# Backward decode attention: dV outer products and the next step's sums interleaved on TensorE, V products made a half quarter ahead

## The chip, the cores and the metric

The kernel runs on one core of a Trainium2 chip. Its time is the device time of one launch in microseconds; lower is better. Five engines work side by side, each taking its own instructions in order: TensorE (PE in the profile, PEld its weight loads), VectorE (DVE), ScalarE (ACT), GpSimd (POOL, used here to issue stores and one kind of load) and SyncE (SP, which issues loads). 16 DMA engines move the data between main memory (HBM) and the on-chip memory (SBUF). TensorE writes into PSUM, from where VectorE and ScalarE read.

## What is computed

One decoding step of a conditioned transformer block, with its gradients. The reference, cut to what matters (all data in bfloat16):

```python
# D = 640, 32 heads, 8192 keys, head size 192
def A_ref(x, k, v, wq, wo):                       # attention, one query row per head
    q = (x @ wq).reshape(B, Sq, 32, 192).transpose(0, 2, 1, 3)
    p = softmax(einsum('bhqd,bhkd->bhqk', q, k) * 192 ** -0.5)
    o = einsum('bhqk,bhkd->bhqd', p, v)
    return o.transpose(0, 2, 1, 3).reshape(B, Sq, 6144) @ wo
mod = (silu(c) @ w_mod).reshape(1, 6, 1, 640)     # sa, ca, ga, sb, cb, gb
x = x + ga * A_ref(layernorm(x) * (1 + ca) + sa, k_cache, v_cache, wq, wo)
x = x + gb * B_ref(layernorm(x) * (1 + cb) + sb)  # a small MLP block
out, vjp = jax.vjp(f, x, k_cache, v_cache, wq, wo, w3, w4, c, w_mod)
return out, *vjp(grad_out)
```

For one head with softmax weights p, output gradient do and query q, the backward pass needs, for every key j: dP_j = V_j . do (a dot product over 192 elements), dS_j = p_j (dP_j - const), dK_j = dS_j q and dV_j = p_j do. The gradients of the caches are as large as the caches: 32 heads x 8192 keys x 192, 100 MB each. V is read a second time for dP; K isn't, since the forward pass keeps what dQ needs.

## The kernel before, in words

The forward part runs over the heads and takes the first 550 us or so. A short chain of small operations follows (the MLP block and its gradients). Then comes the loop to which the change belongs.

**The backward loop.** It has 64 steps (`NS = 2 * HQ`), one for half of the keys of one head, 4096 keys laid out as 128 partitions x 32 keys (`JH`), in two quarters of 16 keys (`JQ`). What a step s does:

- `dot_sum(ps, dP)` (L314, DVE): adds up the last 16 partial sums per key that lie in PSUM: dP of this step. Then dS in one operation (L1156), each value four times.
- `mul_q(s + 1, q)` (L855, DVE): V times do for quarter q of the *next* step, into half q of the buffer `pq`. `tree_q(ps, q)` (L864, PE): 12 matmuls with the identity as weights, which add the 192 products of a key down to 16 in PSUM. One buffer `dot_ps` holds both quarters.
- `dv_groups` (L875, PE): dV. Eight groups a step; each is four matmuls with one row of p as the weights (outer products with do), into one of two PSUM buffers `dv_ps`, and one eviction by ScalarE (L876, 128x768) into a bfloat16 buffer.
- `dk_part` (L880, DVE): dK, in two halves.
- `dv_store` (L1126) and the dK store (L1197) are issued by POOL, as is `load_er` (L704), which fetches the rows of p for step s + 2 into one of two buffers `er_b`. It has to wait until PE is done with the groups of step s. V for step s + 4 is loaded by SP (L295) into one of three buffers, as soon as its last reader, the products of step s + 1, is done.
- dV and dK go into five buffers (named `KB` in the profile, `OB` in the code) that are used in turn.

**Side jobs.** A step has four calls of `slot()`. Each runs a share of a list of small pieces of work: the transposes and products for dWq, dW_mod and dWo, and `g_do`, which makes do of later heads from rows of wo. How many pieces are due by which slot is fixed by a formula; there is no planner. A chunk of dWq or dW_mod goes through `g_chunk` in five pieces: a cast (L943), transposes of a weight chunk (L746, evicted by ACT at L747) together with the transpose of three small rows (L948) and their copy `vrow` (L950), more transposes with a broadcast (L955, evicted at L957), matmuls (L962) with three row products (L964), and an addition (L966) with the last two row products (L968). The loads of weight chunks go through SP (L904, L214), their stores through POOL (L972, L999).

**What sets the order.** The order of the instructions on PE, DVE, ACT and SP is that of the program text (`manual_schedule`); the framework adds the waits that the data need. POOL issues its transfers in the order of the text too. An engine whose next instruction has to wait holds up everything behind it.

The step in the old order: dot_sum, dS, slot, groups 0 to 3, product 0 and its tree, slot, first half of dK, groups 4 and 5, slot, groups 6 and 7, load of er_b, store of dV, product 1 and its tree, V load, second half of dK, store of dK, slot.

Of the kernel before, what the change touches and what calls it, by code (L numbers as in the profile page):

```python
# [10 lines left out]
ALU = mybir.AluOpType  # L11
# [9 lines left out]
def kernel(  # L21
# [26 lines left out]
    nc = tc.nc  # L48
    P = 128
    D = A_x.shape[-1]  # L50
    _, HQ, S, DH = A_k_cache.shape
# [4 lines left out]
    JH = J // 2  # L56
    JQ = J // 4
    TS = 16
    TF = 8
    HW = DH // 2  # L60
    ND = D // P
# [232 lines left out]
    def load_v(h, t, v):  # L294
        nc.sync.dma_start(out=v, in_=V_hd[h][:, t * JH : (t + 1) * JH, :])  # L295
        return v
# [410 lines left out]
    def ht(s):  # L707

        return H1 - s // 2, (1 - s % 2 if s < 2 else s % 2)
# [29 lines left out]
    def transposed(x0, cols, outer, wT):  # L739

        n = min(8, 15 - x0)
        tp = psT.tile([P, 1024], BF16, name="wT_ps", tag="t")
        for x in range(x0, x0 + n):
            b, a = divmod(x, outer)
            for lo, hi, src in cols(a, b):
                T_.transpose(out=tp[lo:hi, (x - x0) * P : (x - x0 + 1) * P], in_=src, identity=ident_bf)  # L746
        A_.copy(out=wT[:, x0 * P : (x0 + n) * P], in_=tp[:, 0 : n * P])  # L747
# [7 lines left out]
    def do_mm(t, b=None):  # L755
        wT = woT[t]
        ps = psB.tile([P, 512], FP32, name="do_ps", tag="b")
        bs = (0, 1) if b is None else (b,)
        w = DH * len(bs)
        for i in range(ND):  # L760
            rhs = wT[:, i * PW : (i + 1) * PW].rearrange("p (c a) -> p c a", c=3)[:, :, 64 * bs[0] : 64 * bs[-1] + 64]
            T_.matmul(ps[:, 0:w], lhsT=dao_bf[:, i : i + 1].to_broadcast([P, P]), rhs=rhs, start=(i == 0), stop=(i == ND - 1))  # L762
        for k, b in enumerate(bs):
            h = 2 * t + b
            A_.activation(
                out=do_of(h).rearrange("p (a c) -> p a c", c=3),
                in_=ps[:, 0:w].rearrange("p (c a) -> p a c", c=3)[:, 64 * k : 64 * k + 64, :],
                func=ACT.Copy,
                scale=rinv[:, h : h + 1],
            )  # L770
# [83 lines left out]
    def mul_q(s, q):  # L854
        V_.tensor_tensor(  # L855
            out=pq[:, q],
            in0=v_l[s][:, q * JQ : (q + 1) * JQ, :],
            in1=do_of(ht(s)[0])[:, None, :].to_broadcast([P, JQ, DH]),
            op=ALU.mult,
        )  # L860

    def tree_q(ps, q):
        for k in range(0, DH, TS):
            T_.matmul(ps[:, q * JQ : (q + 1) * JQ, :], lhsT=ident_bf, rhs=pq[:, q, :, k : k + TS], start=(k == 0), stop=(k == DH - TS), skip_group_check=True)  # L864

    def dv_groups(dV, er, doh, gs):

        dV4 = dV.rearrange("p (r k) d -> p r (k d)", r=4)
        for g in gs:
            m, q = divmod(g, 2)  # L870
            ps = psV.tile([P, 2, 512], FP32, name="dv_ps", tag="v")
            for k in range(2):
                for b in range(2):
                    p0 = 32 * (2 * q + b)
                    T_.matmul(ps[:, b, k * DH : (k + 1) * DH], lhsT=er[p0 : p0 + 1, 2 * m + k, :], rhs=doh[p0 : p0 + 1, :], start=True, stop=True)  # L875
            A_.copy(out=dV4[:, 2 * q : 2 * q + 2, m * PW : (m + 1) * PW], in_=ps[:, :, 0:PW])  # L876

    def dk_part(dK, qh, dS4, lo, hi):
        n = hi - lo
        V_.tensor_tensor(  # L880
            out=dK[:, lo:hi, :].rearrange("p j (a b) -> p j a b", b=4),
            in0=qh.rearrange("p (a b) -> p a b", b=4)[:, None, :, :].to_broadcast([P, n, DH // 4, 4]),
            in1=dS4[:, lo:hi, None, :].to_broadcast([P, n, DH // 4, 4]),
            op=ALU.mult,
        )
# [49 lines left out]
    def g_chunk(b, first, v3, rows, dst, n, acc, lay):  # L935

        lo = n * CW
        if first:
            cur["w"] = cur.pop("next")
        w = stg = cur["w"][:, :, b * PW : (b + 1) * PW]  # L940
        cols = lambda a, b_: [(l, r, w[:, a, c0 : c0 + r - l]) for bb, l, r, c0 in lay if bb == b_]
        v_bf = tcol(3, "v_bf", BF16)
        V_.tensor_copy(out=v_bf, in_=v3)  # L943
        yield
        wT = bst.tile([P, 15 * P], BF16, name="wT", tag="wT")
        transposed(0, cols, ND, wT)
        tp = psS.tile([NF, P], FP32, name="bc_t", tag="s")
        T_.transpose(out=tp[0:3, :], in_=v3, identity=ident_f)  # L948
        vrow = tmp.tile([3, P], BF16, name="vrow")
        V_.tensor_copy(out=vrow, in_=tp[0:3, :])  # L950
        yield
        transposed(8, cols, ND, wT)
        bp = psB.tile([P, 512], FP32, name="bc_ps", tag="b")
        for bb, l, r, c0 in lay:
            T_.matmul(bp[:, c0 : c0 + r - l], lhsT=pick(3, bb), rhs=vrow[:, l:r], start=True, stop=True)  # L955
        v_bc = bst.tile([P, PW], BF16, name="v_bc")
        A_.copy(out=v_bc, in_=bp[:, 0:PW])  # L957
        yield
        ps = psS.tile([P, ND], FP32, name="acc_ps", tag="s")
        for i in range(ND):  # L960
            for bb in range(3):
                T_.matmul(ps[:, i : i + 1], lhsT=wT[:, (bb * ND + i) * P : (bb * ND + i + 1) * P], rhs=v_bf[:, bb : bb + 1], start=(bb == 0), stop=(bb == 2))  # L962
        for i in range(3):
            V_.tensor_scalar(out=stg[:, i, :], in0=v_bc, scalar1=rows[:, i : i + 1], scalar2=None, op0=ALU.mult)  # L964
        yield
        V_.tensor_tensor(out=acc, in0=ps, in1=acc, op=ALU.add)  # L966
        for i in range(3, ND):
            V_.tensor_scalar(out=stg[:, i, :], in0=v_bc, scalar1=rows[:, i : i + 1], scalar2=None, op0=ALU.mult)  # L968
        if first:
            next_w()  # L970
        else:
            nc.gpsimd.dma_start(out=dst[:, :, lo : lo + CW], in_=cur["w"])  # L972
        yield
# [118 lines left out]
    def slot():  # L1092
        prog[0] += 1
        k = prog[0] - 1
        due = sum(n for i, n in RAMP.items() if i <= k) if k < R0 else NR + -(-(NP - NR) * (k - R0 + 1) // (SLOTS - R0))
        while prog[1] < min(due, NP):
            next(side)
            prog[1] += 1

    def v_buf(s):  # L1100
        return KY if s == 0 else VB[(s + 1) % NVB]
# [39 lines left out]
    dw4_store(stg0[:, 2 * D :], 9, 3)  # L1141
    V_.tensor_tensor(out=cpr, in0=c_ps, in1=rinv, op=ALU.mult)
    tree_q(ps, 1)
    V_.memset(dha, 0.0)
    V_.memset(dsc, 0.0)
    row = None
    for s in range(NS):
        h, t = ht(s)
        nxt = s + 1 < NS
        doh = do_of(h)  # L1150
        qh = qs_bc[:, h * DH : (h + 1) * DH]
        assert not nxt or (s + 1) // 4 in done
        dP = tcol(JH, "dP")
        dot_sum(ps, dP)
        dS4 = bst.tile([P, JH, 4], BF16, name="dS4", bufs=2)
        V_.scalar_tensor_tensor(  # L1156
            out=dS4,
            in0=dP[:, :, None].to_broadcast([P, JH, 4]),
            scalar=cpr[:, h : h + 1],
            in1=E_all[:, h, t * JH : (t + 1) * JH, None].to_broadcast([P, JH, 4]),  # L1160
            op0=ALU.subtract,
            op1=ALU.mult,
        )
        slot()
        dV, dK = OB[(2 * s) % len(OB)], OB[(2 * s + 1) % len(OB)]
        if s == 0:
            dv_groups(dV, er, doh, (1, 3))
            do_mm(TL, 0)
        else:
            er = er_l.pop(s)  # L1170
            dv_groups(dV, er, doh, (0, 1, 2, 3))
        if nxt:
            ps = psR.tile([P, JH, TS], FP32, name="dot_ps")
            mul_q(s + 1, 0)
            tree_q(ps, 0)
        if row is not None:
            dq_cols(row)
            row = None
        slot()
        dk_part(dK, qh, dS4, 0, JQ)  # L1180
        if s > 0:
            dv_groups(dV, er, doh, (4, 5))
        slot()
        dv_groups(dV, er, doh, (5, 7) if s == 0 else (6, 7))
        if s + 2 < NS:
            er_l[s + 2] = load_er(s + 2)
        dv_store(s, dV, JQ if s == 0 else 0, JH)
        if nxt:
            mul_q(s + 1, 1)
            tree_q(ps, 1)  # L1190
            v_l.pop(s, None)
        if h == H1:
            row = dq_rows(t, (KD, KE)[t], dS4)
        if s + 4 < NS:
            v_l[s + 4] = load_v(*ht(s + 4), v_buf(s + 4))
        dk_part(dK, qh, dS4, JQ, JH)
        nc.gpsimd.dma_start(out=dK_hd[h][:, t * JH : (t + 1) * JH, :], in_=dK)  # L1197
        done_s[0] = s + 1
        slot()
    while prog[1] < NP:  # L1200
# [32 lines left out]
```

## Time and profile before

| what | value |
|---|---|
| time, median of 3 runs | 1435.73 us (1430.34 to 1438.45) |
| the profiled execution's own time | 1433.26 us |
| its span, first to last instruction | 1431.5 us |
| PE busy | 1105.0 us (77%) |
| DVE busy | 1104.2 us (77%) |
| ACT busy | 871.5 us (61%) |
| bytes moved by DMA | 569.38 MB, mean 398 GB/s |
| mean granted TensorE clock | 0.768 |

How to read it: the page gives, for each engine, the time in which it was busy, and for the span in 40 slices the busy share of each engine in tenths, the TensorE clock that was granted, and what the DMA engines moved. The other views answer for a stretch of the span: busy time and transfer rate by stretch, groups of instructions by line with the idle time ahead of them and what ended it, waits by pair of waiter and awaited, and the instructions in order of time. The first step of the backward loop starts near 593 us, the last one ends near 1420 us.

### The profile page before, as it was taken

To read this page: it belongs to the slowest core of one execution; us is meant where nothing else is said; L and a number is where in the kernel's file an instruction comes from. 1 tells how busy PE (TensorE), PEld (TensorE's weight loads), DVE (VectorE), ACT (ScalarE), POOL (GpSimd) and SP (SyncE) were. 2 spreads that over 40 slices of the span, in tenths; PEclk is the share of its full clock that TensorE was granted. 3 is DMA by queue.
4 is the path that set the end of the run, shared out by engine and by line. 5 is a ranking of instruction groups with operands and counts; after the bars stand their busy time and mean duration, and the time that the engine had idled before them with its cause. 6 is when DMAs were issued, how large, how long until landed. Compare 5 with 4: busy or idle time off the path is not lost.

```text
span 1431.5 us, 30396 instructions
## 1 busy us (share of the span) xinstructions
PE 1105.0 (77%) x12744; PEld 790.1 (55%) x12744; DVE 1104.2 (77%) x1410; ACT 871.5 (61%) x1953; POOL 145.6 (10%) x254
## 2 busy tenths in 40 slices
PE   3988889999999998767757677677777777666864
PEld 2777777777777777634334344444444444344532
DVE  4989999999999996676757677676676676667674
ACT  0767777777777775455646466555565556455554
POOL 0000000000000000111211111111111111111111
PEclk9999999999999998766667575666655555556565
DMA  9999999999999995499999999999999999999998
GB/s 374 391 397 418 415 417 417 412 422 411 420 408 413 418 415 211 164 385 428 422 399 425 427 408 421 416 425 403 425 418 425 402 422 414 358 385 382 422 404 372
DMA packets 77417, 569.38 MB, mean 398 GB/s; under 512 B 8766, under 2 KB 26510, under 8 KB 36958
## 3 DMA queue, kind: packets, MB, share of 16 engines
q1 hardware_dynamic: 50842, 340.44, 59.2%
q0 software_dynamic: 26416, 226.97, 38.0%
q8 instruction: 100, 1.64, 0.5%
q14 instruction: 39, 0.32, 0.1%
q10 hardware_dynamic: 20, 0.00, 0.0%
HBM read 340.95 MB, written 226.43 MB: 396 GB/s over the span
## 4 chain that ended last, share of the span: by engine, by line
PE 26%; DVE 12%; DMA 8%; ACT 8%; issue 4%; POOL 1%; ACTq 0%; POOLq 0%; DVEq 0%; SPq 0%
PE dot_ps L864 17%; DVE pq L855 6%; ACT KB L876 6%; DMA wo_st<-in_A_wo_dram 4%; PE wT_ps L746 3%; PE dv_ps L875 3%; DMA stg<-in_A_wq_dram 2%; ACT wT L747 2%; DMA out_dram<-wo_st 2%; DVE dP L314 2%; DVE KB L880 1%; DMA out_dram<-stg 1%; PE do_ps L762 1%; DVE dq_junk L984 1%; DVE dS L1156 0%
## 5 line engine op out<-in xcount | busy, mean ns | idle before, releaser
L876 ACT CAST KB<-dv_ps 128x768 bf16<-128x768 f32 x512 | 376.3, 815 | 146.9 <-PE dv_ps L875 146.5
L864 PE MATMUL dot_ps<-pq,ident_bf 128*128 128x256 bf16 x1536 | 317.2, 388 | 50.2 <-DVE pq L855 50.1
L357 ACT ACTIVATE vs<-VB,Ef 128x192 bf16<-128x192 bf16 x872 | 314.9, 447 | 0.0
L864 PEld LDWEIGHTS <-ident_bf 128*128 128x128 bf16 x1536 | 198.5, 133 | 146.2 <-issue 77.4
L875 PE MATMUL dv_ps<-do_r,er_b 1*128 1x192 bf16 x2048 | 173.5, 309 | 131.1 <-ACT KB L876 129.9
L300 DVE TENSOR_TENSOR prod<-KB,qs_bc 128x6144 bf16<-128x6144 bf16 x62 | 207.9, 3353 | 30.0 <-DMA KB<-in_A_k_cache_dram 23.0
L880 DVE TENSOR_TENSOR KB<-qs_bc,dS 128x3072 bf16<-128x3072 bf16 x128 | 223.8, 1749 | 4.5 <-DMA out_dram<-KB 4.2
L855 DVE TENSOR_TENSOR pq<-VB,do_r 128x3072 bf16<-128x3072 bf16 x126 | 220.3, 1749 | 0.0
L372 PE MATMUL mp<-vs,KB 128*128 128x193 bf16 x1984 | 191.3, 249 | 4.3 <-ACT vs L357 2.8
L747 ACT COPY wT<-wT_ps 128x1024 bf16<-128x1024 bf16 x84 | 81.0, 964 | 185.4 <-PE wT_ps L746 185.4
L875 PEld LDWEIGHTS <-er_b 1*128 1x128 bf16 x2048 | 65.7, 102 | 223.2 <-issue 220.4
L372 PEld LDWEIGHTS <-KB 128*128 128x128 bf16 x1984 | 171.2, 98 | 13.6 <-DMA KB<-in_A_k_cache_dram 4.7
L310 PE MATMUL half_ps<-prod,ident_bf 128*128 128x256 bf16 x744 | 95.1, 279 | 45.8 <-DVE prod L304 45.4
L314 DVE TENSOR_REDUCE dP<-dot_ps 128x32 f32<-128x512 f32 x64 | 44.0, 688 | 109.8 <-PE dot_ps L864 109.8
L350 DVE TENSOR_TENSOR vs<-VB,E 128x1728 bf16<-128x1728 bf16 (+1 forms) x122 | 127.1, 1062 | 0.3 <-ACT vs L357 0.3
L304 DVE TENSOR_TENSOR prod<-prod 128x3072 bf16<-128x3072 bf16 x62 | 108.7, 1753 | 1.0
L310 PEld LDWEIGHTS <-ident_bf 128*128 128x128 bf16 x744 | 72.8, 99 | 64.1 <-issue 55.0
L377 PE MATMUL mp<-vs,KB 128*64 128x193 bf16 x1984 | 108.0, 252 | 0.0
L377 PEld LDWEIGHTS <-KB 128*64 128x64 bf16 x1984 | 80.8, 111 | 19.8 <-issue 19.7
L337 ACT ACTIVATE E<-S_h,negm 128x256 bf16<-128x256 f32 x31 | 15.8, 508 | 116.0 <-DVE negm L498 113.7
L704 POOL DMA_DIRECT2D er_b<-eT_d x64 | 37.3, 583 | 476.1 <-PE dv_ps L875 474.3
L432 POOL DMA_DIRECT2D eT_d<-er x16 | 8.8, 548 | 560.1 <-ACT vs L348 519.7
(270 smaller groups left out, 1008.5 us busy)
## 6 DMA issues: line engine op xcount, KB each, us to landing
out_dram<-KB POOLq DMA_DIRECT2D x127, 1536.0 KB, 15.6
VB<-in_A_v_cache_dram SPq DMA_DIRECT2D x123, 1536.0 KB, 11.6
KB<-in_A_k_cache_dram SPq DMA_DIRECT2D x64, 1536.0 KB, 11.6
wo_st<-in_A_wo_dram SPq DMA_DIRECT2D x31, 480.0 KB, 12.1
w_st<-in_A_wq_dram SPq DMA_DIRECT2D x12, 960.0 KB, 13.5
out_dram<-wo_st POOLq DMA_DIRECT2D x16, 480.0 KB, 18.8
out_dram<-w_st POOLq DMA_DIRECT2D x7, 960.0 KB, 16.4
w_st<-in_w_mod_dram SPq DMA_DIRECT2D x6, 960.0 KB, 18.2
```

Of the source, the lines that this page charges most:

```text
L300: V_.tensor_tensor(out=prod, in0=src, in1=vec[:, None, :].to_broadcast([P, JH, DH]), op=ALU.mult)
L310: T_.matmul(ps, lhsT=ident_bf, rhs=prod[:, :, k : k + TF], start=(k == 0), stop=(k == w - TF))
L350: V_.tensor_tensor(out=vs[:, 0:n, 0:DH].rearrange("p j (a b) -> p j a b", b=4), in0=v[:, v0 : v0 + n, :].rearrange("p j (a b) -> p j a b", ...
L357: A_.activation(out=vs[:, k, 0:DH], in_=v[:, v0 + k, :], func=ACT.Copy, scale=Ef[:, j0 + k : j0 + k + 1])
L372: T_.matmul(mp[:, 0:MW], lhsT=kb[:, j0 + k, 0:P], rhs=vs[:, k, 0:MW], start=(q == 0 and k == 0), stop=(z and k == JQ - 1), skip_group_chec ...
L377: T_.matmul(mp[p0 : p0 + 64, MO : MO + MW], lhsT=kb[:, j0 + k, P:DH], rhs=vs[:, k, 0:MW], start=False, stop=(z and k >= JQ - 2), skip_grou ...
L747: A_.copy(out=wT[:, x0 * P : (x0 + n) * P], in_=tp[:, 0 : n * P])
L855: V_.tensor_tensor(out=pq[:, q], in0=v_l[s][:, q * JQ : (q + 1) * JQ, :], in1=do_of(ht(s)[0])[:, None, :].to_broadcast([P, JQ, DH]), op=AL ...
L864: T_.matmul(ps[:, q * JQ : (q + 1) * JQ, :], lhsT=ident_bf, rhs=pq[:, q, :, k : k + TS], start=(k == 0), stop=(k == DH - TS), skip_group_c ...
L875: T_.matmul(ps[:, b, k * DH : (k + 1) * DH], lhsT=er[p0 : p0 + 1, 2 * m + k, :], rhs=doh[p0 : p0 + 1, :], start=True, stop=True)
L876: A_.copy(out=dV4[:, 2 * q : 2 * q + 2, m * PW : (m + 1) * PW], in_=ps[:, :, 0:PW])
L880: V_.tensor_tensor(out=dK[:, lo:hi, :].rearrange("p j (a b) -> p j a b", b=4), in0=qh.rearrange("p (a b) -> p a b", b=4)[:, None, :, :].to ...
```

## The change

Within a step, the order of the work on the engines changes; no operation is added or taken away.

- Each dV group on PE is followed by some of the sums of the next step: four matmuls each after groups 1, 2 and 3 (quarter 0), three each after groups 4 to 7 (quarter 1). `tree_q` takes the range as arguments.
- Product 0 is made two steps ahead, at the end of the step (`mul_q(s + 2, 0)`, and `mul_q(1, 0)` ahead of the loop); product 1 of the next step is made after the first slot.
- The load of V for step s + 4 follows product 1, ahead of groups 2 to 7.
- Both halves of dK come in the middle of the step, and its store is issued there, ahead of the er_b load and the store of dV.
- The first step, of which four groups were made ahead of the loop, has its other four at places 0, 1, 4 and 6.
- In `g_chunk` the three small rows are transposed ahead of the wide transposes, their copy `vrow` moves to the next piece, and all five row products stand in the last piece.

```diff
@@ -859,8 +859,8 @@
             op=ALU.mult,
         )
 
-    def tree_q(ps, q):
-        for k in range(0, DH, TS):
+    def tree_q(ps, q, lo=0, hi=DH // TS):
+        for k in range(lo * TS, hi * TS, TS):
             T_.matmul(ps[:, q * JQ : (q + 1) * JQ, :], lhsT=ident_bf, rhs=pq[:, q, :, k : k + TS], start=(k == 0), stop=(k == DH - TS), skip_group_check=True)
 
     def dv_groups(dV, er, doh, gs):
@@ -943,12 +943,12 @@
         V_.tensor_copy(out=v_bf, in_=v3)
         yield
         wT = bst.tile([P, 15 * P], BF16, name="wT", tag="wT")
-        transposed(0, cols, ND, wT)
         tp = psS.tile([NF, P], FP32, name="bc_t", tag="s")
         T_.transpose(out=tp[0:3, :], in_=v3, identity=ident_f)
+        transposed(0, cols, ND, wT)
+        yield
         vrow = tmp.tile([3, P], BF16, name="vrow")
         V_.tensor_copy(out=vrow, in_=tp[0:3, :])
-        yield
         transposed(8, cols, ND, wT)
         bp = psB.tile([P, 512], FP32, name="bc_ps", tag="b")
         for bb, l, r, c0 in lay:
@@ -960,11 +960,9 @@
         for i in range(ND):
             for bb in range(3):
                 T_.matmul(ps[:, i : i + 1], lhsT=wT[:, (bb * ND + i) * P : (bb * ND + i + 1) * P], rhs=v_bf[:, bb : bb + 1], start=(bb == 0), stop=(bb == 2))
-        for i in range(3):
-            V_.tensor_scalar(out=stg[:, i, :], in0=v_bc, scalar1=rows[:, i : i + 1], scalar2=None, op0=ALU.mult)
         yield
         V_.tensor_tensor(out=acc, in0=ps, in1=acc, op=ALU.add)
-        for i in range(3, ND):
+        for i in range(ND):
             V_.tensor_scalar(out=stg[:, i, :], in0=v_bc, scalar1=rows[:, i : i + 1], scalar2=None, op0=ALU.mult)
         if first:
             next_w()
@@ -1141,6 +1139,7 @@
     dw4_store(stg0[:, 2 * D :], 9, 3)
     V_.tensor_tensor(out=cpr, in0=c_ps, in1=rinv, op=ALU.mult)
     tree_q(ps, 1)
+    mul_q(1, 0)
     V_.memset(dha, 0.0)
     V_.memset(dsc, 0.0)
     row = None
@@ -1149,7 +1148,6 @@
         nxt = s + 1 < NS
         doh = do_of(h)
         qh = qs_bc[:, h * DH : (h + 1) * DH]
-        assert not nxt or (s + 1) // 4 in done
         dP = tcol(JH, "dP")
         dot_sum(ps, dP)
         dS4 = bst.tile([P, JH, 4], BF16, name="dS4", bufs=2)
@@ -1161,40 +1159,62 @@
             op0=ALU.subtract,
             op1=ALU.mult,
         )
-        slot()
         dV, dK = OB[(2 * s) % len(OB)], OB[(2 * s + 1) % len(OB)]
+        gs = [0, 1, 2, 3, 4, 5, 6, 7]
         if s == 0:
-            dv_groups(dV, er, doh, (1, 3))
-            do_mm(TL, 0)
+            gs = [1, 3, None, None, 5, None, 7, None]
         else:
             er = er_l.pop(s)
-            dv_groups(dV, er, doh, (0, 1, 2, 3))
         if nxt:
             ps = psR.tile([P, JH, TS], FP32, name="dot_ps")
-            mul_q(s + 1, 0)
-            tree_q(ps, 0)
+
+        def dv(k):
+            if gs[k] is not None:
+                dv_groups(dV, er, doh, (gs[k],))
+
+        def tree(q, lo, hi):
+            if nxt:
+                tree_q(ps, q, lo, hi)
+
+        dv(0)
+        dv(1)
+        slot()
+        if s == 0:
+            do_mm(TL, 0)
+        tree(0, 0, 4)
+        if nxt:
+            mul_q(s + 1, 1)
+            v_l.pop(s + 1, None)
+        if s + 4 < NS:
+            v_l[s + 4] = load_v(*ht(s + 4), v_buf(s + 4))
+        dv(2)
+        tree(0, 4, 8)
+        dv(3)
+        tree(0, 8, 12)
         if row is not None:
             dq_cols(row)
             row = None
+        dk_part(dK, qh, dS4, 0, JQ)
         slot()
-        dk_part(dK, qh, dS4, 0, JQ)
-        if s > 0:
-            dv_groups(dV, er, doh, (4, 5))
+        dv(4)
+        tree(1, 0, 3)
+        dk_part(dK, qh, dS4, JQ, JH)
+        nc.gpsimd.dma_start(out=dK_hd[h][:, t * JH : (t + 1) * JH, :], in_=dK)
+        dv(5)
+        tree(1, 3, 6)
         slot()
-        dv_groups(dV, er, doh, (5, 7) if s == 0 else (6, 7))
+        dv(6)
+        tree(1, 6, 9)
+        dv(7)
         if s + 2 < NS:
             er_l[s + 2] = load_er(s + 2)
         dv_store(s, dV, JQ if s == 0 else 0, JH)
-        if nxt:
-            mul_q(s + 1, 1)
-            tree_q(ps, 1)
-            v_l.pop(s, None)
+        tree(1, 9, 12)
         if h == H1:
             row = dq_rows(t, (KD, KE)[t], dS4)
-        if s + 4 < NS:
-            v_l[s + 4] = load_v(*ht(s + 4), v_buf(s + 4))
-        dk_part(dK, qh, dS4, JQ, JH)
-        nc.gpsimd.dma_start(out=dK_hd[h][:, t * JH : (t + 1) * JH, :], in_=dK)
+        if s + 2 < NS:
+            assert (s + 2) // 4 in done
+            mul_q(s + 2, 0)
         done_s[0] = s + 1
         slot()
     while prog[1] < NP:
```

## The prediction

> **What bounds the kernel now.** The page first: its span and, of the 40 slices, the share of time for which the 16 DMA engines were busy (tenths) and what they moved.
>
> ```profile
> span 1431.5 us, 30396 instructions
> DMA  9999999999999995499999999999999999999998
> GB/s 374 391 397 418 415 417 417 412 422 411 420 408 413 418 415 211 164 385 428 422 399 425 427 408 421 416 425 403 425 418 425 402 422 414 358 385 382 422 404 372
> ```
>
> The change lies in the backward loop, slices 17 to 40. DMA is busy in all of them, but the rate wanders between 358 and 428 GB/s. So the second view is busy time by stretches: the start of the loop, its body, a stretch at the best rate, a long stretch, a stall, a late stretch and the tail.
>
> ```profile
> 592.00:640.00 48.00, 32.02 (x346) 20.62 (x345) 36.34 (x36) 28.76 (x43) 7.74 (x14) 0.82 0.87 328
> 640.00:1420.00 780.00, 555.55 (x4595) 335.77 (x4593) 543.81 (x782) 437.81 (x614) 124.28 (x211) 0.62 1.00 411
> 660.00:680.00 20.00, 15.08 (x113) 8.83 (x113) 13.22 (x13) 11.31 (x18) 2.19 (x4) 0.59 1.01 427
> 964.00:1200.00 236.00, 175.73 (x1455) 107.68 (x1454) 164.85 (x248) 136.44 (x193) 36.28 (x61) 0.61 1.01 416
> 1217.50:1237.60 20.10, 9.62 (x84) 5.45 (x83) 10.22 (x20) 6.82 (x9) 2.79 (x5) 0.50 0.86 344
> 1240.00:1380.00 140.00, 101.73 (x860) 62.46 (x858) 101.76 (x168) 76.75 (x106) 22.12 (x36) 0.59 1.00 394
> 1420.00:1431.50 11.50, 0.00 (x0) 0.00 (x0) 0.00 (x0) 0.00 (x0) 0.70 (x2) 0.50 0.68 284
> ```
>
> Columns after the length: busy PE, PEld, DVE, ACT, POOL, then granted clock, DMA share, GB/s. The body takes 780 us; no engine is over 71% busy there (PE 555.55). The transfer view of the same stretch, and the rows of its groups:
>
> ```profile
> DMA packets 42712, 320.68 MB, mean 411 GB/s; under 512 B 5510, under 2 KB 14038, under 8 KB 20083
> ```
> ```profile
> L876 ACT CAST KB<-dv_ps 128x768 bf16<-128x768 f32 x476 | 349.7, 816 | 133.2 <-PE dv_ps L875 132.9
> L864 PE MATMUL dot_ps<-pq,ident_bf 128*128 128x256 bf16 x1413 | 296.8, 393 | 43.6 <-DVE pq L855 43.5
> L880 DVE TENSOR_TENSOR KB<-qs_bc,dS 128x3072 bf16<-128x3072 bf16 x120 | 209.8, 1749 | 4.5 <-DMA out_dram<-KB 4.2
> L855 DVE TENSOR_TENSOR pq<-VB,do_r 128x3072 bf16<-128x3072 bf16 x117 | 204.6, 1748 | 0.0
> L875 PE MATMUL dv_ps<-do_r,er_b 1*128 1x192 bf16 x1904 | 162.4, 311 | 123.1 <-ACT KB L876 122.5
> L314 DVE TENSOR_REDUCE dP<-dot_ps 128x32 f32<-128x512 f32 x59 | 40.6, 687 | 102.7 <-PE dot_ps L864 102.7
> ```
>
> L314 runs once a step, so the body holds 59 steps of 780/59 = 13.2 us. Per step PE is busy 555.55/59 = 9.4, DVE 543.81/59 = 9.2, ACT 437.81/59 = 7.4 us. At 427 GB/s the 320.68 MB need 320.68/0.427 = 751 us, 12.7 us a step. So two limits lie close together: transfers at 12.7, and a chain through three engines that hand work to each other, at 13.2 with its stalls. The waits say who hands to whom (waiter, awaited, total us, times, longest):
>
> ```profile
> PE dv_ps L875 <- ACT KB L876: 122.5, 203, 1.6
> DVE dP L314 <- PE dot_ps L864: 102.7, 47, 14.0
> DVE vrow L950 <- PE bc_t L948: 59.4, 19, 8.5
> PE dot_ps L864 <- DVE pq L855: 43.5, 51, 2.2
> PE wT_ps L746 <- DMA wo_st<-in_A_wo_dram: 22.6, 4, 12.2
> DVE w_st L964 <- ACT v_bc L957: 17.6, 7, 4.0
> DVE stg L964 <- ACT v_bc L957: 15.2, 8, 3.9
> PE wT_ps L746 <- DMA stg<-in_A_wq_dram: 7.3, 1, 7.3
> DVE KB L880 <- DMA out_dram<-KB: 4.2, 3, 3.1
> ```
>
> Waits on transfers sum to 22.6 + 7.3 + 4.2 = 34 us; waits between engines are ten times that. In 1240:1380 the engines set the pace: 394 GB/s, though the DMA share reads 1.00. I read that as packets that take longer when few are queued, so the rate, not the share, shows the loss. The body loses 780 − 751 = **29 us** against the best rate.
>
> The Trainium skill ("DMA: Bandwidth & Descriptors", Specifications) gives a fabric ceiling of 435 GB/s and an HBM limit of about 358 GB/s per core. The row with 427 contradicts the second and comes close to the first; by 435 the loss would be 780 − 737 = 43 us. I stay with 427, which a row shows.
>
> **The change, part by part.** It adds and removes no instruction; each moves.
>
> *Interleaving.* Before, PE runs dV groups in pairs and 12 sums (a "tree") in one go. One clean step, PE alone:
>
> ```profile
> 1404.84 0.34 PE L875 MATMUL dv_ps<-do_r,er_b 1*128 1x192 bf16 x4 [0.92 <-ACT KB L876]
> 1405.54 0.34 PE L875 MATMUL dv_ps<-do_r,er_b 1*128 1x192 bf16 x4 [0.36 <-ACT KB L876]
> 1406.30 1.49 PE L864 MATMUL dot_ps<-pq,ident_bf 128*128 128x256 bf16 x12 [0.43 <-DVE pq L855]
> 1409.17 0.50 PE L875 MATMUL dv_ps<-do_r,er_b 1*128 1x192 bf16 x4 [0.94 <-ACT KB L876]
> 1410.31 2.74 PE L864 MATMUL dot_ps<-pq,ident_bf 128*128 128x256 bf16 x12
> ```
>
> A group's PSUM buffer (two exist) comes free after an eviction; PE waits up to 0.94 for it. With 3 or 4 sums behind each group, 0.37 to 0.91 us of PE work (1.49/12 × 3 to 2.74/12 × 4) stands between two groups; over two groups that covers one eviction (816 ns) and most of its hand-over. I put 122.5 us at about a third of itself: 80 us of PE waits go. They lie on PE's path, which ends the step.
>
> PE's floor per step is then 8 groups + 24 sums + the rest. The rest is 555.55 − 296.8 − 162.4 = 96.4, /59 = 1.6 us. On the fast durations: 8×0.34 + 2×1.49 + 1.6×0.62 = 6.7 us. On the slow ones: 8×0.50 + 2×2.74 + 1.6×0.62/0.5 = 11.5 us. Both ends are below the transfers' 12.7.
>
> *V products a half quarter ahead.* Product 0 of step s+2 is made at the end of step s, product 1 of s+1 at the start, three groups and 12 sums ahead of its tree. The 43.5 us wait of L864 goes. DVE does the same two products of 1.75 us a step; what hides them is DVE's 13.2 − 9.2 = 4.0 us of idle time. If that cover were gone, each would cost 1.75. What is late next: dP, which waits for the last three sums, and then only for PE.
>
> *dK behind.* Both halves (2 × 1749 ns) move to mid-step; dK's store goes out before the er_b load and before dV's store. On POOL, er_b(s+2) now stands behind a store issued some 4 us earlier instead of a step earlier. The store's size and V load's, and landing times of er_b and of the dK store:
>
> ```profile
> out_dram<-KB POOLq DMA_DIRECT2D x127, 1536.0 KB, 15.6
> VB<-in_A_v_cache_dram SPq DMA_DIRECT2D x123, 1536.0 KB, 11.6
> ```
> ```profile
> DMA to landing us min/median/max: 3.6/10.2/16.2
> DMA to landing us min/median/max: 9.5/18.3/25.0
> ```
>
> One more 1.57 MB store ahead costs er_b 3.7 us (all the rate) to 7.4 (half of it): landing 13.9 to 17.6, against one step of time until its first dV group. So er_b may become a wait. It can last only while the ring in front is full of stores, that is, while the transfers are the bound; I cost it at 0, with −0 and +41 us (59 × 0.7, 13.9 less 13.2) as ends.
>
> *V load earlier.* On SP the load of V(s+4) follows product 1, so it goes about half a step earlier, and passes the weight loads of two slots. A weight load can then land one V load later, 1.57/0.427 = 3.7 us; five waits on weights (4 + 1 rows) make that +18 at worst, 0 at best, where SP's earlier release brings them forward as much. I take +4, one such delay, since these waits are few.
>
> *Side jobs' rows first.* The 3-row transpose precedes the wide ones and vrow's copy moves a slot on: DVE's 59.4 goes. The five row products go together one slot later: 17.6 + 15.2 = 32.8 goes. These 92 us are 1.6 us a step of DVE idle time, in front of dP and the products.
>
> **The sum.** Engines lose about 80 + 43.5 us of PE waits and 92 of DVE waits, partly the same microseconds. The larger side alone, 123 us, is 2.1 a step: 13.2 − 2.1 = 11.1 us, under 12.7. So the transfers take over, and no more than 29 us can come back. By stretches: 1240:1380 loses 140 × (1 − 394/427) = 10.8, paced by the engines: all back. 964:1200 loses 236 × (1 − 416/427) = 6.1 and the remainder 29 − 10.8 − 6.1 − 3.9 = 8.2: two thirds, 9.5, since restarts after load stalls stay. The stall at 1217 loses 20.1 × (1 − 344/427) = 3.9: stays. Weight delay +4. Body: −10.8 − 9.5 + 4 = −16.3.
>
> Start and tail:
>
> ```profile
> 593.50 0.69 DVE L314 TENSOR_REDUCE dP<-dot_ps 128x32 f32<-128x512 f32 x1 [3.35 <-PE dot_ps L864]
> 594.50 1.75 DVE L855 TENSOR_TENSOR pq<-VB,do_r 128x3072 bf16<-128x3072 bf16 x1
> 1419.65 0.53 POOL L1126 DMA_DIRECT2D out_dram<-KB  x1 [6.76 <-ACT KB L876]
> 1420.17 0.53 POOL L1197 DMA_DIRECT2D out_dram<-KB  x1
> ```
>
> The product at 594.50 moves into the 3.35 us of idle time before dP: −1.75. The last dK store leaves some 2 us ahead of dV's instead of 0.5 behind it; the ring still needs its bytes' time: −1 (ends 0 and −2.5). Total −19: 1433.26, the profiled execution's own time (span 1431.5 and 1.8 around it), becomes 1414. The median of the runs shown is 1435.73, 2.5 above: **1417 us**, own range 1402 (all 29 + 4) to 1428.
>
> **The rivals.**
> - *The gain is hidden* (0.22). Engines get faster, but DMA share is already 1.00; they run into weight and er_b waits sooner, each draining the stores as at 1217 (3.9 us). Four such more cost 16: 1433. For it: longest waits on wo_st of 12.2 us. Against it: 394 GB/s over 140 us without such a wait.
> - *er_b behind dK* (0.09), slower. If er_b's landing exceeds a step while the ring runs dry between stores, PE waits at the first dV group: from 13.2 us of landing on it decides, and at 13.9 it costs 59 × 0.7 = 41 less the 16 gained: 1433 + 25 = 1458. Against it: a landing that late needs a full ring, which is the best rate.
> - *PE stays on its slow clock and keeps waiting for evictions* (0.08), slower. 11.5 + 122.5/59 = 13.6 us a step, 0.4 over 13.2: 59 × 0.4 = +24, 1457. It decides from 13.2. For it: granted clock 0.62. The Trainium skill ("TensorE: Matmul & The Clock Gate", A second HAM failure mode) says that brief idle gaps between groups make the clock fall back and rise again, which gives this time if more and shorter gaps replace the long ones; the trace agrees that both clocks occur.
>
> **How the numbers follow.** Forecast 0.57, hidden 0.22, the two slower ones 0.17, and 0.04 for transfers better than 427. About 0.5%, 7.2 us, is what a measurement here can tell from no change: faster 0.60, same 0.22, slower 0.18. The range 1402 to 1441 takes in the forecast and the hidden case and leaves out the slower ones.
>
> **What would show it.** After: rate in the body near 420, above 415 in the late stretch; vrow, L964 and L864's waits on DVE near nothing; L875's wait on ACT under 60; waits on transfers (wo_st, er_b, stores) larger; DVE idle before dP. The forecast is wrong if the body's rate stays at 411 with engine waits gone (hidden), if PE waits on er_b at lower rates, or if PE is busy over 11 us a step at a clock near 0.5.

## The result, and the profile after

The changed kernel takes **1423.12 us** (median of 4 runs, 1420.24 to 1424.9) against 1434.68 us for the kernel before (4 runs): ratio 0.9923, 95% interval 0.9898 to 0.9949. The forecast was 1417 us against 1435.73, a gain of 19; the gain is 11.6. The profiled execution has a span of 1418.5 us, 13.0 less than before.

The page of the changed kernel, its span and the granted TensorE clock in 40 slices:

```profile
span 1418.5 us, 30477 instructions
PEclk7899999999999998655555555555555555665555
```

Busy time by stretch (busy PE, PEld, DVE, ACT, POOL, then granted clock, DMA share, GB/s), changed kernel:

```profile
592.00:640.00 48.00, 42.90 (x356) 21.16 (x353) 38.87 (x37) 30.86 (x45) 7.77 (x16) 0.65 0.94 375
640.00:1200.00 560.00, 457.20 (x3286) 217.04 (x3286) 386.92 (x551) 329.87 (x446) 89.11 (x153) 0.53 1.01 418
1217.50:1237.60 20.10, 13.23 (x108) 5.93 (x105) 14.94 (x32) 9.54 (x13) 2.22 (x4) 0.58 1.02 426
1240.00:1340.00 100.00, 82.29 (x660) 41.10 (x657) 73.80 (x122) 60.34 (x81) 15.67 (x27) 0.55 1.01 416
1340.00:1380.00 40.00, 31.43 (x211) 13.34 (x210) 24.92 (x32) 21.78 (x29) 6.49 (x11) 0.50 0.95 375
1380.00:1406.00 26.00, 22.91 (x149) 8.26 (x148) 20.98 (x17) 17.96 (x24) 4.37 (x8) 0.50 0.96 401
1406.00:1418.50 12.50, 0.52 (x5) 0.13 (x3) 0.00 (x0) 1.61 (x3) 1.07 (x2) 0.50 0.69 287
```

The same view of the kernel before, for the stretches that the prediction does not show:

```profile
640.00:1200.00 560.00, 400.78 (x3316) 243.40 (x3316) 388.92 (x555) 317.33 (x449) 89.54 (x153) 0.63 1.01 418
1240.00:1340.00 100.00, 71.97 (x615) 44.66 (x612) 72.84 (x128) 54.44 (x75) 15.69 (x25) 0.59 1.00 390
1340.00:1380.00 40.00, 29.76 (x247) 17.80 (x246) 28.92 (x40) 22.32 (x31) 6.43 (x11) 0.59 1.01 405
1380.00:1420.00 40.00, 27.51 (x220) 14.50 (x219) 29.28 (x23) 25.75 (x36) 6.36 (x12) 0.63 0.99 419
```

Read the last column against the one before. From 640 to 1200 us both kernels move 418 GB/s: the long middle of the loop gained nothing. The gain lies at its ends: the start (328 to 375), the stall at 1217 (344 to 426) and 1240:1340 (390 to 416). From 1340 on its rate is the lower one (375 where the other had 405), but by then it is some 15 us ahead, so these windows hold different work; the steps are compared further down. The clock column tells a second thing: PE is busy for 457 instead of 401 us in the middle, for the same work, because its clock fell from 0.63 to 0.53.

The groups of the body, changed kernel, 640 to 1406 us (busy us, mean ns, idle time in front and what ended it):

```profile
L864 PE MATMUL dot_ps<-pq,ident_bf 128*128 128x256 bf16 x1394 | 354.0, 397 | 3.8 <-DVE dP L314 3.1
L875 PE MATMUL dv_ps<-do_r,er_b 1*128 1x192 bf16 x1884 | 207.5, 337 | 83.2 <-DMA er_b<-eT_d 79.3 <-ACT KB L876 3.2
L880 DVE TENSOR_TENSOR KB<-qs_bc,dS 128x3072 bf16<-128x3072 bf16 x118 | 203.8, 1753 | 135.9 <-DMA out_dram<-KB 88.7 <-issue 38.6 <-DMA er_b<-eT_d 7.3
L314 DVE TENSOR_REDUCE dP<-dot_ps 128x32 f32<-128x512 f32 x59 | 40.6, 689 | 65.6 <-PE dot_ps L864 65.2
```

Every engine wait that the change aimed at is gone: L875 on evictions 122.5 to 3.2 us, L864 on products 43.5 to nothing that shows; vrow and the row products no longer stand among the waits of DVE (PE now waits 5.1 us for vrow). In their place stand two waits on transfers: 79.3 us on er_b and 88.7 us on output buffers that are not yet stored (4.2 before). The engines got out of the transfers' way and now run into them.

### The profile page after: what moved, and what is told of

It is laid out like the page before. It is cut to its first block, busy times and chain, and to the rows that moved or that the text cites. A ratio compares the mean times of both kernels' runs of the same rounds, so it can differ in the third digit from the quotient of the medians.

```text
span 1418.5 us, 30477 instructions
## 1 busy us (share of the span) xinstructions
PE 1186.6 (84%) x12744; PEld 750.6 (53%) x12744; DVE 1103.0 (78%) x1410; ACT 892.9 (63%) x1953; POOL 144.3 (10%) x254
## 4 chain that ended last, share of the span: by engine, by line
DMA 23%; issue 16%; PE 15%; POOL 3%; DVE 1%; ACT 1%; POOLq 0%; DVEq 0%; ACTq 0%; SPq 0%
DMA er_b<-eT_d 12%; PE dot_ps L864 7%; PE dv_ps L875 4%; DMA w_st<-in_A_wq_dram 4%; DMA wo_st<-in_A_wo_dram 3%; DMA out_dram<-KB 2%; PE wT_ps L746 2%; DMA out_dram<-wo_st 2%; DMA out_dram<-w_st 1%; POOL er_b L704 1%; POOL out_dram L1124 1%; POOL out_dram L1202 1%; PE do_ps L762 1%; DVE KB L880 0%; PE w3T_ps L725 0%
## 5 line engine op out<-in xcount | busy, mean ns | idle before, releaser
L876 ACT CAST KB<-dv_ps 128x768 bf16<-128x768 f32 x512 | 396.0, 804 | 211.6 <-PE dv_ps L875 210.1
L864 PE MATMUL dot_ps<-pq,ident_bf 128*128 128x256 bf16 x1536 | 383.7, 393 | 7.9 <-DVE dP L314 6.8
L875 PE MATMUL dv_ps<-do_r,er_b 1*128 1x192 bf16 x2048 | 224.3, 335 | 83.9 <-DMA er_b<-eT_d 79.3
L864 PEld LDWEIGHTS <-ident_bf 128*128 128x128 bf16 x1536 | 153.0, 123 | 160.5 <-issue 121.8
L855 DVE TENSOR_TENSOR pq<-VB,do_r 128x3072 bf16<-128x3072 bf16 x126 | 220.5, 1750 | 14.7 <-PE dot_ps L864 12.7
L875 PEld LDWEIGHTS <-er_b 1*128 1x128 bf16 x2048 | 66.2, 104 | 235.9 <-issue 145.4
L310 PEld LDWEIGHTS <-ident_bf 128*128 128x128 bf16 x744 | 73.1, 100 | 62.9 <-issue 53.3
L1202 POOL DMA_DIRECT2D out_dram<-KB x64 | 35.3, 552 | 469.8 <-DVE KB L880 308.5
## 6 DMA issues: line engine op xcount, KB each, us to landing
KB<-in_A_k_cache_dram SPq DMA_DIRECT2D x64, 1536.0 KB, 11.6
wo_st<-in_A_wo_dram SPq DMA_DIRECT2D x31, 480.0 KB, 12.3
w_st<-in_A_wq_dram SPq DMA_DIRECT2D x12, 960.0 KB, 12.7
```

The costliest lines, as they stand in the source:

```text
L310: T_.matmul(ps, lhsT=ident_bf, rhs=prod[:, :, k : k + TF], start=(k == 0), stop=(k == w - TF))
L855: V_.tensor_tensor(out=pq[:, q], in0=v_l[s][:, q * JQ : (q + 1) * JQ, :], in1=do_of(ht(s)[0])[:, None, :].to_broadcast([P, JQ, DH]), op=AL ...
```

## The experiments

Two theories were set against each other. **T**: the changed kernel is bound by transfers in nearly all of the loop, and the waits on er_b and on the buffers are back pressure. **E**: the engines, at the low clock, are the bound, and those waits only lie beside it. A step's mean length is read from the first and last start of dS, of which there is one a step, 63 intervals apart.

### Transfers taken away: b_quarter, a_quarter, p_quarter

```diff
-        dma_start(out=dK_hd[h][:, t * JH : (t + 1) * JH, :], in_=dK)
+        dma_start(out=dK_hd[h][:, t * JH : t * JH + JH // 4, :], in_=dK[:, 0 : JH // 4, :])
-        dma_start(out=dV_hd[h][:, t * JH + lo : t * JH + hi, :], in_=dV[:, lo:hi, :])
+        dma_start(out=dV_hd[h][:, t * JH + lo : t * JH + lo + (hi - lo) // 4, :], in_=dV[:, lo : lo + (hi - lo) // 4, :])
```

Kernel before, b_quarter:

> The kernel before, but of every dK and dV store only a quarter of the keys goes out (8 of 32 per partition; three quarters of dK and dV are left out of the output). All engine work stays. This takes the transfers away as a bound: about 3.0 MB a step, 7 us at 427 GB/s. Theory T (the changed kernel is bound by transfers; before, engines and transfers lay close together): the engines' own pace shows, 12 to 12.6 us a step in place of 13.2, so 1375 to 1400 us. Rival E (the engines at a low TensorE clock are the bound in both kernels, and the waits on transfers only lie beside them): within 1% of before.

Changed kernel, a_quarter:

> The changed kernel with the same cut (a quarter of dK and dV stored, the rest left out). Theory T: the engines' pace is 10.5 to 11.5 us a step in place of 13.0, so 1290 to 1340 us, and clearly under the kernel before with the same cut. Rival E: 12.3 us or more a step, over 1385 us.

Changed kernel without the interleaving (groups in pairs, sums in twelves), p_quarter:

> The changed kernel in pairs (no interleaving) with a quarter of dK and dV stored and the rest left out, against the interleaved one with the same cut (11.2 us a step between steps 14 and 48, 1297 us). If the interleaving makes the engines faster and the transfers only hide it: 11.8 to 12.5 us a step, 1330 to 1375 us, with PE waits on evictions back at 80 us or more. If the lower clock takes back what the missing waits give: 10.8 to 11.5 us a step, 1285 to 1310 us.

Times: 1397.91 us (ratio 0.975, 0.969 to 0.981), 1297.33 (0.905, 0.903 to 0.907) and 1292.5 (0.903, 0.894 to 0.911). The line of dS (durations, then first and last start in us) of before, changed, b_quarter, a_quarter and p_quarter, one fence each:

```profile
L1156 DVE SCALAR_TENSOR_TENSOR dS<-dP,cpr,E_all x64: 350/352/353, 594.2 to 1413.8; 128x128 bf16<-128x128 f32 x64
```
```profile
L1154 DVE SCALAR_TENSOR_TENSOR dS<-dP,cpr,E_all x64: 350/352/353, 591.9 to 1402.1; 128x128 bf16<-128x128 f32 x64
```
```profile
L1156 DVE SCALAR_TENSOR_TENSOR dS<-dP,cpr,E_all x64: 350/352/353, 593.0 to 1393.2; 128x128 bf16<-128x128 f32 x64
```
```profile
L1154 DVE SCALAR_TENSOR_TENSOR dS<-dP,cpr,E_all x64: 350/352/353, 592.3 to 1286.3; 128x128 bf16<-128x128 f32 x64
```
```profile
L1154 DVE SCALAR_TENSOR_TENSOR dS<-dP,cpr,E_all x64: 350/352/354, 589.6 to 1284.7; 128x128 bf16<-128x128 f32 x64
```

That is (last − first)/63 = 13.0, 12.9, **12.7, 11.0 and 11.0** us a step. With full transfers the two kernels differ by 0.15 us a step; freed of them, by 1.7 (the other run of b_quarter was 14 us shorter, which would make it 1.5). So the change did shorten the engines' own step by 12 to 13%, and the transfers hide nearly all of it: E is out, its 12.3 us a step isn't there. The kernel before had its engines at 12.7, a little over T's 12 to 12.6 and just under the 13.0 that a step takes with full transfers.

p_quarter settles what the interleaving gives to that pace: without it the engines are as fast. Busy time from 640 to 1200 us, a_quarter and then p_quarter, with the same number of matmuls:

```profile
640.00:1200.00 560.00, 520.94 (x3951) 255.29 (x3951) 463.16 (x692) 389.14 (x528) 105.38 (x181) 0.58 0.80 282
```
```profile
640.00:1200.00 560.00, 447.21 (x3947) 273.03 (x3947) 461.44 (x690) 371.48 (x526) 108.50 (x179) 0.66 0.79 279
```

PE is busy for 74 us more in the interleaved order, at a clock of 0.58 against 0.66. In pairs it waits instead, in this stretch:

```profile
PE dv_ps L875 <- ACT KB L876: 67.0, 137, 1.2
```

67 us of waits on one side, 74 us of longer PE work at the slower clock on the other: the two nearly cancel.

### Engine work taken away: a_half, b_half

```diff
         for k in range(lo * TS, hi * TS, TS):
-            T_.matmul(ps[...], lhsT=ident_bf, rhs=pq[:, q, :, k : k + TS], start=(k == 0), stop=(k == DH - TS), ...)
+            if k % (2 * TS) == 0:
+                T_.matmul(ps[...], lhsT=ident_bf, rhs=pq[:, q, :, k : k + TS], start=(k == 0), stop=(k == DH - 2 * TS), ...)
```

> The changed kernel with every second of the 12 sums per quarter left out (so dP, dS and dK are not the reference's): 12 matmuls a step less on TensorE, 2.7 us a step at the low clock, all transfers kept. Theory T: no gain in the body, up to 8 us in the five last steps, which have no loads: 1413 to 1423 us. Rival E: 2 us or more a step, under 1330 us.

> The kernel before with every second sum left out in the same way. Theory T: its engines get out of the transfers' way as the change does, so it comes to the changed kernel's time, 1410 to 1425 us. Rival E: 60 us or more off, under 1375 us.

Measured: 1417.59 us (0.9886, 0.9871 to 0.9902) and 1422.57 us (0.9920, 0.9901 to 0.9939). With half of the sums away, the changed kernel gains 0.4%, hardly clear of the noise (the intervals overlap a little), and the kernel before comes to the changed kernel's ratio. From 640 to 1200 us, a_half and then b_half:

```profile
640.00:1200.00 560.00, 374.81 (x2807) 154.02 (x2808) 386.35 (x557) 331.27 (x450) 89.42 (x153) 0.50 1.01 419
```
```profile
640.00:1200.00 560.00, 332.76 (x2803) 182.03 (x2805) 389.89 (x560) 317.66 (x449) 89.78 (x154) 0.52 1.01 420
```

419 and 420 GB/s, where the full kernels have 418: with PE busy for 67% and 59% of the time, the stretch is no faster. For this mix of transfers that is the ceiling (the highest of any run here is b_mul's 422), not the 427 of a single good slice.

### One part alone: b_rows, b_mul

The side jobs' edit alone, put into the kernel before (b_rows), and the V products alone (b_mul):

```diff
# b_mul, against the kernel before
+    mul_q(1, 0)
...
-            mul_q(s + 1, 0)
             tree_q(ps, 0)
+            mul_q(s + 1, 1)
...
-            mul_q(s + 1, 1)
             tree_q(ps, 1)
...
+        if s + 2 < NS:
+            mul_q(s + 2, 0)
         dk_part(dK, qh, dS4, JQ, JH)
```

> The kernel before with the side jobs' edit alone (three small rows transposed first, vrow's copy and the row products a piece later). It frees up to 92 us of DVE idle time. Theory T: any relief of the engines of half a microsecond a step gives most of the gain in the late stretch, but not that at the start: 1424 to 1431 us. Rival I: 1432 to 1437 us, no gain.

> The kernel before with the V products alone made ahead (quarter 1 of the next step where quarter 0 was made, quarter 0 of the step after next where quarter 1 was); groups in pairs, dK, V load and rows as before. Theory P (the products are the part that takes the engines off the transfers' path): the sums' waits on products (43 us) go and the time comes to 1415 to 1427 us, most of the whole change. Rival R (it takes all parts together): 1428 to 1436 us.

Measured: 1427.44 us (0.9962, 0.9947 to 0.9977) and 1424.09 us (0.9938, 0.9908 to 0.9968). Either edit alone gives a gain, 0.4% and 0.6% against the 0.8% of all together. Both fit T: there is a small margin, and any relief of the engines uses it up. These two runs don't show it, since within their intervals the parts could as well add; that more relief brings hardly more is shown by a_half and b_half. The products alone can't be told from the whole change.

### One part undone: a_pairs, a_mulold

```diff
# a_pairs, against the changed kernel
-        tree(0, 0, 4)
...
         dv(2)
-        tree(0, 4, 8)
         dv(3)
-        tree(0, 8, 12)
+        tree(0, 0, 12)
...                                   # and the same for quarter 1, behind group 7
# a_mulold, against the changed kernel
-    mul_q(1, 0)
...
+            mul_q(s + 1, 0)
         tree(0, 0, 4)
-        if nxt:
-            mul_q(s + 1, 1)           # and the V load behind it
...
         dk_part(dK, qh, dS4, 0, JQ)
+        if nxt:
+            mul_q(s + 1, 1)           # and the V load behind it
         slot()
         dv(4)
...
-            mul_q(s + 2, 0)
```

> The changed kernel without the interleaving: groups in pairs and the 12 sums of a quarter in one go, as before; product, dK, V load and rows stay changed. Theory T: PE's waits for evictions come back (80 to 125 us) but stay hidden by the transfers: 1420 to 1431 us. Rival I (the interleaving carries the gain): 1430 to 1440 us. The granted clock in the body tells whether the interleaving lowered it: if so, it comes back from 0.54 to about 0.62.

> The changed kernel with the V products made where they were: quarter 0 of the next step after the first slot, quarter 1 ahead of group 4, the V load behind it; interleaving, dK and rows stay changed. Theory T: waits of the sums on the products come back (40 us or more) and stay mostly hidden: 1420 to 1430 us, with 1 to 4 us lost at the start and in the last steps. Rival M (the products carry the gain): 1431 us or more.

Measured: a_pairs 1417.55 us (0.9904, 0.9879 to 0.9930), a_mulold **1448.05 us** (1.0108, 1.0088 to 1.0127). The stretch from 640 to 1200 us and the waits in it, a_pairs first:

```profile
640.00:1200.00 560.00, 396.40 (x3310) 236.56 (x3306) 388.17 (x557) 318.35 (x451) 89.94 (x153) 0.62 1.01 419
...
PE dv_ps L875 <- ACT KB L876: 55.6, 114, 1.2
```
```profile
640.00:1200.00 560.00, 462.03 (x3231) 216.49 (x3228) 383.59 (x542) 328.28 (x442) 87.86 (x151) 0.53 1.00 408
...
PE dot_ps L864 <- DVE pq L855: 60.9, 34, 4.1
```

Undoing the interleaving costs nothing (the two intervals overlap; the median is lower), and the clock comes back to 0.62. Undoing the products costs 1.8%: I had given this 1431 us or more as the rival, and the rival holds. With the interleaving the low clock makes PE's path long; where PE then also waits for products, the engines fall behind the transfers (408 GB/s). PE's busy time and this one wait fill 523 of the 560 us, and in the same stretch the waits on transfers are nearly gone: 2.3 us on er_b and 8.4 on output buffers, where the changed kernel has 65.2 and 84.8. The V load, which this edit moves with the product, is nowhere waited for. The same old products with sums in twelves gave 1427 us (b_rows). That points to a price of the interleaving that the products ahead pay for, but it isn't shown: b_rows also leaves dK and the V load where they were.

### The er_b wait: a_er_act, and both: c1, c2

```diff
-        nc.gpsimd.dma_start(out=er[0:P:32, :, :]...
+        nc.scalar.dma_start(out=er[0:P:32, :, :]...
```

> The changed kernel with the er_b load issued by ScalarE in place of POOL, so that it no longer stands behind the dK store in POOL's queue; nothing else moves. Theory T (the er_b wait is back pressure of full transfer queues): er_b lands within 8 us, the 79 us of waits on it fall under 15 us, waits on the output buffers grow in their place, and the time stays within 6 us of the changed kernel, 1417 to 1429 us. Rival W (the er_b wait costs time of its own): 15 us or more faster, under 1408 us.

> The changed kernel with groups in pairs and sums in twelves as before, and the er_b load issued by ScalarE: the two variants that were 0.4% faster each, together. If both gains are of the same microseconds (transfers full either way): 1414 to 1419 us. If they add: 1409 to 1413 us.

> As c1, but interleaved from the sixth last step on, where no weights are loaded and the engines set the pace (9.6 us a step interleaved, 10.3 in pairs). Expected 2 to 3 us under c1, if the steps at the end are on the path and the clock there is low in either order; the same as c1 if not.

Measured: a_er_act 1417.65 us (0.9895, 0.9875 to 0.9914); **c1 1414.63 us** (0.9860, 0.9835 to 0.9885); c2 1415.43 us (0.9878, 0.9850 to 0.9907). In a_er_act the 73.9 us that PE waits for er_b between 640 and 1340 us in the changed kernel (first fence) are gone, and the wait on output buffers grows from 85.9 to 118.8 (second fence):

```profile
DVE KB L880 <- DMA out_dram<-KB: 85.9, 24, 7.1
...
PE dv_ps L875 <- DMA er_b<-eT_d: 73.9, 25, 6.0
```
```profile
DVE KB L880 <- DMA out_dram<-KB: 118.8, 33, 8.6
```

That is back pressure changing its place, as T has it, with at most 0.4% of time, which the intervals can't separate from none. The Trainium skill ("Trainium Kernel Development and Optimization", Key Constraints) says that all issuing queues share the same 16 DMA engines and that issuing from several saves only the sequencer's issue time; here another queue also took a small load out from behind the stores, and a wait of 73.9 us went, so the trace does not agree with the "only". c1, pairs and er_b on ScalarE, is the one version with the whole output that is faster than the changed kernel by intervals that lie clear of each other. Against a_pairs and a_er_act alone its interval overlaps a little, so whether their gains are the same microseconds or add stays open. One place where it gains on the changed kernel is the start:

```profile
592.00:640.00 48.00, 36.62 (x355) 22.63 (x354) 39.84 (x39) 29.41 (x45) 5.89 (x11) 0.71 1.00 402
```

402 GB/s at the start of the loop, where the changed kernel has 375 and the kernel before 328. The pairs alone reach it (a_pairs has 406 there). c2, interleaved at the end only, brought nothing over c1, though 2 to 3 us were expected if the end were on the path.

## Why the prediction was right, and where its sizes were off

*The bound.* Right: transfers take over once the engines lose a little time. The forecast for the engines was 13.2 − 2.1 = 11.1 us a step; a_quarter shows 11.0. That the two agree so well is partly luck. 80 of the 123 us behind the 2.1 were the interleaving's, and p_quarter has 11.0 without it. The start was too high as well: 780/59 counts 59 starts in a stretch that holds 60 steps, a step before took 13.0, and the engines alone needed 12.7, so they gained 1.7 and not 2.1. (The same count makes the transfers' 12.7 a 12.5. And slice 17, which the prediction counts to the loop, lies mostly ahead of it: 164 GB/s.) That the kernel before lay close at both limits holds too (12.7 for the engines alone).

*What could come back: 29 us.* This is the term that was mis-sized. It rests on 427 GB/s, the rate of one good slice of 20 us. The mix with weight chunks gives 418 to 422 even when PE is idle for 41% of the time (b_half, 420), so of 964:1200 and "the remainder", for which I put −9.5 us, nothing came: 418 before, 418 after, from 640 to 1200 us. For this long middle the rival *The gain is hidden* describes what happened better than the forecast: the engines' waits went and waits on er_b and the stores took their place. From 640 to 1406 us the rate is 415, where the sign was to be "near 420"; and the waits on wo_st, which were to grow, fell from 22.6 to 10.9 us.

*The terms one by one*, a rate's difference turned into time at 418 GB/s:

| term | predicted, us | measured, us | from |
|---|---|---|---|
| start | −1.75 | −5.4 | 48 × 47/418; 2.3 of it show at the first dS |
| middle of the body | −9.5 | 0 | 418 and 418 GB/s |
| stall at 1217 | 0 | −3.9 | 20.1 × 82/418 |
| 1240:1340 | −10.8 (to 1380) | −6.2 | 100 × 26/418 |
| from 1340 to the end | −1, and the rest of the line above | +4.9 | 396 GB/s over the last 91.5 us before, 370 over 78.5 after: 78.5 × 26/418 |
| weight delay | +4 | about 0 | below |

The sum is −10.6 of the span's −13.0. These windows are stretches of time, and late in the loop the two kernels are at different places in the work. Counted by steps nothing is left over. The start of dS in steps 47, 50, 58 and 59 (of 0 to 63), the kernel before first, then the changed kernel:

```profile
1205.14 0.35 DVE L1156 SCALAR_TENSOR_TENSOR dS<-dP,cpr,E_all 128x128 bf16<-128x128 f32 x1
1253.14 0.35 DVE L1156 SCALAR_TENSOR_TENSOR dS<-dP,cpr,E_all 128x128 bf16<-128x128 f32 x1
1361.18 0.35 DVE L1156 SCALAR_TENSOR_TENSOR dS<-dP,cpr,E_all 128x128 bf16<-128x128 f32 x1
1374.52 0.35 DVE L1156 SCALAR_TENSOR_TENSOR dS<-dP,cpr,E_all 128x128 bf16<-128x128 f32 x1
```
```profile
1203.18 0.35 DVE L1154 SCALAR_TENSOR_TENSOR dS<-dP,cpr,E_all 128x128 bf16<-128x128 f32 x1
1240.80 0.35 DVE L1154 SCALAR_TENSOR_TENSOR dS<-dP,cpr,E_all 128x128 bf16<-128x128 f32 x1
1343.28 0.35 DVE L1154 SCALAR_TENSOR_TENSOR dS<-dP,cpr,E_all 128x128 bf16<-128x128 f32 x1
1363.51 0.35 DVE L1154 SCALAR_TENSOR_TENSOR dS<-dP,cpr,E_all 128x128 bf16<-128x128 f32 x1
```

The changed kernel is ahead by 2.3 us at the first dS, 2.0 at step 47 (on the way it swings between −5.5 and 7.5), 12.3 at step 50, 17.9 at step 58, 11.0 at step 59, 11.7 at the last dS and 13.0 at the end. So the start and the long middle together gave 2.0, the three steps around the stall 10.3, and the eight steps behind them 5.6. Step 58 alone lost 6.9. The rest gave 2.0, of which 1.3 is the tail (17.7 us from the last dS to the end before, 16.4 after), where −1 was forecast. That the total came within 7 us of the forecast is therefore partly luck too: the 9.5 of the middle didn't come and step 58 cost 6.9, but the steps around the stall gave 10.3 where its 3.9 had been left standing, and the weight delay of 4 stayed away.

The late stretch came back as argued, since there the engines were the pace: relieved in another way, it rises as well (b_half has 406 GB/s from 1240 to 1340 us, against 390). The stall, which I left standing, went from the rate, not from PE: PE still waits 4.6 us for a weight chunk there (7.3 before), while the transfers run on at 426 GB/s. What I missed is step 58, 20.2 us against 13.3 before. PE waits 5.2 us for er_b, and DVE stands still for 9.6 in front of dK, for which the view names no awaited instruction (both in the changed kernel's waits from 1342 to 1363 us); what holds DVE there stays open.

```profile
DVE KB L880 <- issue: 9.6, 1, 9.6
...
PE dv_ps L875 <- DMA er_b<-eT_d: 5.2, 1, 5.2
```

*Interleaving: 80 us of PE waits go.* They went, 119 us even, and it was worth nothing: the clock took it back (p_quarter). The prediction put PE's floor between 6.7 us a step on the fast clock and 11.5 on the slow one; the changed kernel is busy for 457.20/560 of a step of 12.9, 10.5 us, close to the slow end. Rows of one step and the first group of the next, PE alone, show it: the groups at the slow 0.50, the tree pieces at 1.03 for four sums and 0.82 for three, and a gap only where er_b is awaited:

```profile
966.70 0.50 PE L875 MATMUL dv_ps<-do_r,er_b 1*128 1x192 bf16 x4
967.13 1.03 PE L864 MATMUL dot_ps<-pq,ident_bf 128*128 128x256 bf16 x4
972.28 0.50 PE L875 MATMUL dv_ps<-do_r,er_b 1*128 1x192 bf16 x4
972.71 0.82 PE L864 MATMUL dot_ps<-pq,ident_bf 128*128 128x256 bf16 x3
979.53 0.51 PE L875 MATMUL dv_ps<-do_r,er_b 1*128 1x192 bf16 x8 [3.62 <-DMA er_b<-eT_d]
```

The slow-clock rival thus had its clock right and its waits wrong: evictions no longer hold PE up, so it did not come to 13.6.

*V products ahead.* Right in what goes (43.5 us); larger in worth than I thought, as a_mulold shows: without them and the earlier V load this order is slower than the kernel before.

*dK behind, and er_b.* The wait came where it was forecast, at the first dV group (3.62 in the row above). Its landing, in the changed kernel's body:

```profile
DMA to landing us min/median/max: 3.4/12.9/20.2
```

12.9 us in the median against 10.2 before, under the 13.9 to 17.6 that one more store ahead was to cost. It cost at most a little: without that wait a_er_act is 0.3 to 0.4% faster, not clear of the noise.

*V load earlier: +4.* Not seen: PE's waits on weights are the two rows below and 4.6 us on stg, 30.5 together, against 29.9 before.

```profile
PE wT_ps L746 <- DMA w_st<-in_A_wq_dram: 15.0, 2, 9.2
...
PE wT_ps L746 <- DMA wo_st<-in_A_wo_dram: 10.9, 2, 10.7
```

*Side jobs' rows first.* Right: DVE's waits are gone, and the part alone gives 0.4% (b_rows).

## What to carry to other kernels

Before sizing a gain, measure the ceiling of the stretch itself: cut the engine work in half and look at the rate (here 419 and 420 GB/s, not the best slice's 427), and cut the transfers to see the engines' own pace; two such runs told more than all the waits. Where two limits lie within 3% of each other, relief of one can win no more than the distance to the other. Filling an engine's gaps is worth something only if its clock stays: compare the granted clock and the busy time of the same instructions, not the waits that went. And compare two kernels step by step, since equal windows of time hold different work once one is ahead.

## What the runs showed of the hardware

- In these runs TensorE's clock went with the length of the unbroken runs of sums (L864), not with how busy it was. From 640 to 1200 us the granted clock is 0.61 to 0.66 in all eight kernels whose sums come mostly in twelves (before, b_rows, b_mul, b_quarter, a_pairs, p_quarter, c1, c2), with PE busy for 67 to 80% of the time. It is 0.50 to 0.58 in all six whose runs are of six or fewer (after, a_er_act, a_mulold, a_quarter, a_half, b_half), busy for 59 to 93%. Twice the order alone was changed: 82% busy at 0.53 against 71% at 0.62 (the changed kernel and a_pairs), and 93% at 0.58 against 80% at 0.66 in the quarter-store runs. b_half shows that a low clock needs no filled gaps: with runs of six and PE busy for only 59%, it is 0.52. That is a pattern over these runs; idle time, run length and the share of single-row matmuls change together in them.
- The Trainium skill ("TensorE: Matmul & The Clock Gate", Part 1: The HAM clock gate) says that some 3.4 us of sustained activity release the clock and that idle time brings it back. If busy time is what counts as activity, the denser order would run faster, and the trace does not agree (82% busy at 0.53 against 71% at 0.62). That the single-row matmuls (L875) between short runs of sums count as little activity would fit, but no run here separates it.
- A DMA share of 1.00 or 1.01 went with anything from 390 to 428 GB/s: the share does not show how fast the transfers go. The 40 us with 375 GB/s at a share of 0.95 hold the long step 58.
